# The second MLP's output product, by Strassen's scheme instead of directly

## The chip, the cores and the metric

The kernel runs on one core of a Trainium2 chip. The metric is the device time of one execution in microseconds (us), as a median of runs. TensorE (PE) multiplies matrices, VectorE (DVE) and ScalarE (ACT) do elementwise work and read the results from PSUM, GpSimd (POOL) does elementwise work in SBUF and issues some DMAs, and SyncE (SP) issues most DMAs. Every engine works through its own queue in order.

## What is computed

Attention with a small set of packed queries in the middle, then two MLPs in a row, all in float32 (the weights arrive as float64 words and are converted on the chip):

```
p_packed = softmax(p k^T / 8) v                    # 8 batches, 8 heads, 32 packed rows, head size 64
x  = softmax(q p_packed^T / 8) p_packed            # -> 4608 tokens x 512
h  = x @ w_in                                      # 512 -> 2048
g  = where(h >= 1, h, where(h <= -1, 0, (h + 1)**2 / 4))
y  = g @ w_out                                     # 2048 -> 512
h2 = y @ w2_in                                     # 512 -> 2048
g2 = h2 * sigmoid(h2)
out = g2 @ w2_out                                  # 2048 -> 512
```

## The kernel before

Every float32 product is made of three passes: each operand is split into a high part (ScalarE's cast to the type that TensorE multiplies) and a low part (VectorE subtracts the high part from the value), and TensorE adds high x high, high x low and low x high (`PASSES`) in PSUM.

The program is one list of events, each with a position (`ev`, `at`), sorted and issued in that order; the order of an engine's queue is that of the list. Attention and the first MLP fill 256 steps, up to some 770 us. In the midst of them the input weights of the second MLP are prepared: by pairs of 128 rows (`a_first` to `a_fourth`, `split_a`) they are added and subtracted as one level of Strassen's scheme in Winograd's form asks, split into high and low, and stored to `a_dram`, seven tiles of 256 KB for each of 8 pairs.

The second MLP goes through 6 blocks of 768 tokens. A block's activations `y` are read as four quarters (two halves of the 512 features by two halves of 384 tokens), summed into seven operands and split (`b_side`, `split_b`). Then, for each of the 8 pairs p of hidden tiles, `b_product` multiplies seven weight sums (`load_a`, one tile each, loaded some seven products ahead) with the seven operands: 7 x 2 x 3 = 42 matmuls of 384 columns into two banks, out of which `c_sum` adds the four quarters of the hidden tiles (c11, c21, c12, c22: hidden tile 1 or 2, tokens 1 or 2), with VectorE reading one operand from PSUM. `c_sig` and `c_mult` make x * sigmoid(x), `c_hi` and `c_lo` split it, and `b_out` (L784) multiplies it directly with two tiles of the output weights: tokens are the stationary operand, 512 output features the moving one, 36 matmuls of 512 columns per pair, summed over all pairs in six banks, copied out with tokens on the partitions (L794, L796) and stored (L803). The output weights are converted and split during the first blocks (`conv_a`, `conv_b`, `conv_c`) and stay in SBUF.

The large tiles (weights, operands, splits) share one pool of 37 buffers, `big`; a weight sum's tile is 2 KB per partition.

Of the kernel before, what the change touches and what calls it, by code (L numbers as in the profile page):

```python
# [17 lines left out]

# [60 lines left out]
def attention_then_two_mlps(ctx: ExitStack, tc: tile.TileContext, kT, vv, qT, pT, w_in, w_out, w2_in, w2_out, out):  # L79

# [18 lines left out]
    NT = out.shape[0]  # L99
# [10 lines left out]
    TC = TH // P  # L110
# [31 lines left out]
    a_dram = dram.tile([NPR, 7, P, 2, KH * P], F32, name="a_dram")  # L142

# [484 lines left out]

    def split_a(p, w, j, step):

        n = 1 if step is None else 2
        w = w[:, 512 - n * KH * P:]
        t = big.tile([P, 2, n, KH * P], F32R, tag="big", name="a2w")
        lin = t.rearrange("p i j c -> p i (j c)")  # L640
# [24 lines left out]

    def a_fourth(p):
        split_a(p, w_t.pop(("i2", 2 * p)), 3, 3)
        w_t.pop(("i2", 2 * p + 1))

    a_t, yr_t, b_t = {}, {}, {}  # L670

    def load_a(n):
        if n < 7:
            t = big.tile([P, 2, KH * P], F32R, tag="big", name="a2r")
        elif n % 7 in (4, 5):
            t = wk.tile([P, 2, KH * P], F32R, tag="ysb", name="a2r", bufs=2)
# [12 lines left out]
    def split_b(i, j, src):  # L689
        for a in range(KH):  # L690
            t = big.tile([P, 2, TH], F32R, tag="big", name="y2")
            nc.scalar.copy(t[:, 0], src[:, a])
            nc.vector.tensor_tensor(t[:, 1], src[:, a], t[:, 0].bitcast(F32), op=ALU.subtract)
            b_t[i, j, a] = t

    def b_side(i, j):
        b11, b12, b21, b22 = (yr_t[i, k, t] for k in range(2) for t in range(2))
        if j == 0:
            split_b(i, 0, b11)
            nc.vector.tensor_tensor(b11, b12, b11, op=ALU.subtract)  # L700
        elif j == 1:
            t2 = pools["y"].tile([P, KH, TH], F32, tag="yr", name="yt2", bufs=5)
            nc.vector.tensor_tensor(t2, b22, b11, op=ALU.subtract)
            split_b(i, 1, t2)
            yr_t[i, "t2"] = t2
        elif j == 2:
            split_b(i, 2, b21)
        elif j == 3:
            nc.vector.tensor_tensor(b12, b22, b12, op=ALU.subtract)
            split_b(i, 3, b12)  # L710
        elif j == 4:
            split_b(i, 4, b11)
        elif j == 5:
            nc.vector.tensor_tensor(b21, b21, yr_t[i, "t2"], op=ALU.subtract)
            split_b(i, 5, b21)
        else:
            split_b(i, 6, b22)

    bk, sb, c_t = {}, {}, {}

    def b_product(q, j):
        i, p = divmod(q, NPR)
        if j < 2:
            bk[q, j] = bank("ps_h2")
        ps, w = bk[q, j % 2][:, :TH], a_t.pop(7 * q + j)
        n = 0
        for a in range(KH):
            y = b_t[i, j, a] if p + 1 < NPR else b_t.pop((i, j, a))
            for x, k in PASSES:
                nc.tensor.matmul(  # L730
                    ps, w[:, x, a * P:(a + 1) * P], y[:, k, :], start=(n == 0 and j in (0, 1, 3, 4)),
# [7 lines left out]
    def c_sum(q, name):  # L739
        x, y = bk[q, 0][:, :TH], bk.get((q, 1))  # L740
        if name == "p1":
            sb[q, name] = t = tmp(name, 1)
            nc.scalar.copy(t, x)
            return
        y = y[:, :TH]
        ps, other = {
            "u2": (y, "p1"), "u3": (y, "u2"), "c22": (x, "u3"), "c21": (y, "u2"), "c12": (x, "u2"),
        }[name]
        t = tmp(name if name[0] == "u" else "c", 1 if name[0] == "u" else 2)
        nc.vector.tensor_tensor(t, ps, sb[q, other], op=ALU.add)  # L750
# [8 lines left out]
    def c_mult(q, name):
        u, src = c_t[q, name]  # L760
        nc.vector.tensor_tensor(u, src, u, op=ALU.mult)  # L761

    def c_hi(q, name):
        g = big.tile([P, 2, TH], F32R, tag="big", name="g2")
        nc.scalar.copy(g[:, 0], c_t[q, name][0])  # L765
        g_t[q, name] = g

    def c_lo(q, name):
        g = g_t[q, name]
        nc.vector.tensor_tensor(g[:, 1], c_t.pop((q, name))[0], g[:, 0].bitcast(F32), op=ALU.subtract)  # L770

    o_acc = {}

    def b_out(q):
        i, p = divmod(q, NPR)
        order = ((0, 0), (1, 0), (1, 1), (0, 1)) if q + 1 < NPR * NBK else ((0, 0), (1, 1), (1, 0), (0, 1))
        cells = [(f, t, c, x) for f, t in order for c in range(TC) for x in PASSES]
        for f, t, c, (x, k) in cells:
            first, last = p == 0 and f == t, p == NPR - 1 and f != t
            if first and (x, k) == PASSES[0]:  # L780
                o_acc[t, c] = bank("ps_o") if t and c else ps_a.tile([P, DM], F32, tag="acc", name="ps_o")
            ps = o_acc[t, c]
            g, w = g_t[q, f"c{f + 1}{t + 1}"], w_t["o2", 2 * p + f]
            nc.tensor.matmul(  # L784
                ps, g[:, x, c * P:(c + 1) * P], w[:, k, :],
                start=(first and (x, k) == PASSES[0]), stop=(last and (x, k) == PASSES[-1]),
            )
            if last and (x, k) == PASSES[-1]:
                if t and c < 2 and q + 1 < NPR * NBK:
                    osb = big.tile([P, DM], F32, tag="big", name="osb")  # L790
                else:
                    osb = pools["b"].tile([P, DM], F32, tag="osb", name="osb", bufs=3)
                if c == 1 or c == 2 and t:
                    nc.scalar.copy(osb, ps)  # L794
                else:
# [35 lines left out]
    with tc.manual_schedule():  # L831
# [178 lines left out]
        for p in range(NPR):  # L1010
            n = G['ai'] + G['ad'] * p
            for x in range(2):
                key = ("i2", 2 * p + x)
                at(n + 2 * x, load_raw, key)
                at(n + 2 * x + 3, conv_a, key)
                at(n + 2 * x + 4, conv_b, key)
            for x, fn in enumerate((a_first, a_second, a_third, a_fourth)):
                at(n + 8 + x, fn, p)

        def kb(q, j=0):  # L1020
            return NA - 3.95 + 7 * q + j

        for m in range(KF):
            key = ("o2", m)
            n = NA - 8 + m if m < 4 else kb(m // 2 - 1) + 3.5
            ev(n - 4, load_raw, key)
            ev(n, conv_a, key)
            ev(n + (1 if m < 4 else 0.02), conv_b, key)
            ev(n + (2 if m < 4 else 0.04), conv_c, key)
        for i in range(NBK):  # L1030
            n = kb(i * NPR)
            for k in range(2):
                for t in range(2):
                    ev((NA - 31.4 if i == 0 else n - 22) + 2 * k + t, load_y, i, k, t)
            for j in range(7):
                if i == 0:
                    at(NA - 26 + 3 * j, b_side, i, j)
                else:
                    ev(n + 7 * (-2, -1, -1, -1, 0, 0, 0)[j] + 3.6 + 0.01 * j, b_side, i, j)
        for n in range(7 * NPR * NBK):  # L1040
            ev(kb(0, n) - (3 if n < 7 else 6.6) + 0.39, load_a, n)

        chain = {
            1: [(c_sum, "p1", 0)],
            2: [(c_sum, "u2", 0)],
            3: [(c_sig, "c11", 0), (c_mult, "c11", 1), (c_sum, "u3", 2), (c_hi, "c11", 3), (c_lo, "c11", 4)],
            5: [(c_sum, "c22", 0), (c_sig, "c22", 1)],
# [76 lines left out]
```

## Time and profile before

| | us |
|---|---|
| median of 3 runs | 1531.75 (1530.99 to 1532.3) |
| span of the profiled execution, first to last instruction | 1530.2 |
| TensorE busy in it | 1512.8 |
| VectorE, ScalarE, GpSimd busy | 875.1, 743.4, 85.3 |
| mean granted TensorE clock | 0.998 of full speed |

The profiled execution is one of its own; its whole device time isn't given, so its span stands beside the median of the runs, 1.55 us above it. A busy engine is one with an instruction under way; matmuls overlap, so the mean time of one is longer than the distance from one to the next.

### The profile page before, as it was taken

What the parts mean: (1) busy time and instruction counts of PE and PEld (TensorE: products, weight loads), DVE (VectorE), ACT (ScalarE), POOL (GpSimd) and SP (SyncE); (2) the same over time, 40 slices, a digit from 0 to 9 for tenths busy, and PEclk for the clock granted to TensorE, in tenths of its full rate; (3) what the DMA queues carried; (4) which work ended last, traced back from release to release, by engine and by line L of the source; (5) the groups of instructions that cost most, each with busy time, mean ns of one, the idle gap of its engine ahead of it and who ended that gap; (6) DMA issues with size and microseconds to landing.
All of it is one profiled execution on the core that took longest, in us unless ns stands there. A gap on an engine that the chain in (4) does not pass through costs nothing.

```text
span 1530.2 us, 27671 instructions
## 1 busy us (share of the span) xinstructions
PE 1512.8 (99%) x10546; PEld 1380.4 (90%) x10546; DVE 875.1 (57%) x1831; ACT 743.4 (49%) x1665; POOL 85.3 (6%) x132
## 2 busy tenths in 40 slices
PE   8999999999999999999999999999999999999998
PEld 6788999989899899999998989999898989899997
DVE  5886565564746555575666664564364456447343
ACT  4775657565665656666754442343243334224232
POOL 1430000000000000000000010010001001001000
PEclk9999999999999999999999999999999999999999
DMA  9564545252445252432255653535444445445341
GB/s 333 178 222 141 187 132 169 100 166 102 139 157 169 89 182 70 167 116 92 99 179 187 214 165 108 175 122 161 138 137 146 136 147 160 123 151 173 103 138 62
DMA packets 136723, 226.99 MB, mean 148 GB/s; under 512 B 24336, under 2 KB 70416, under 8 KB 136592
## 3 DMA queue, kind: packets, MB, share of 16 engines
q1 hardware_dynamic: 127120, 192.19, 38.5%
q0 software_dynamic: 9472, 33.04, 6.6%
q8 instruction: 84, 1.38, 0.4%
q14 instruction: 47, 0.39, 0.1%
HBM read 186.25 MB, written 38.93 MB: 147 GB/s over the span
## 4 chain that ended last, share of the span: by engine, by line
PE 92%; DVE 2%; ACT 1%; issue 0%; DMA 0%; SPq 0%; DVEq 0%; ACTq 0%
PE ps_o L784 26%; PE ps_y L604 25%; PE ps_h L730 23%; PE ps_h L569 12%; PE ps_wp L497 2%; PE ps_s L420 2%; PE ps_pp L369 1%; PE ps_tr L457 1%; PE ps_wp L485 0%; DVE raw L168 0%; PE ps_s L275 0%; PE ps_et L334 0%; DVE w L169 0%; ACT u L578 0%; DVE u L584 0%
## 5 line engine op out<-in xcount | busy, mean ns | idle before, releaser
L604 PE MATMUL ps_y<-g,w_o 128*128 128x288 f32 x3072 | 459.8, 299 | 2.1 <-POOL g L594 1.8
L604 PEld LDWEIGHTS ps_y<-g,w_o 128*128 128x128 f32 x3072 | 421.3, 189 | 29.5 <-ACT u L578 15.1
L784 PE MATMUL ps_o<-w_o,g 128*128 128x512 f32 x1728 | 401.4, 390 | 0.0
L784 PEld LDWEIGHTS ps_o<-w_o,g 128*128 128x128 f32 x1728 | 324.1, 188 | 65.5
L730 PE MATMUL ps_h<-y,a2r 128*128 128x384 f32 x2016 | 362.6, 337 | 0.0
L730 PEld LDWEIGHTS ps_h<-y,a2r 128*128 128x128 f32 x2016 | 354.7, 188 | 3.7
L750 DVE TENSOR_TENSOR c<-ps_h,u 128x384 f32<-128x384 f32 x144 | 80.3, 558 | 313.0 <-PE ps_h L730 308.0
L756 ACT ACTIVATE s<-c 128x384 f32<-128x384 f32 x144 | 75.8, 526 | 370.1 <-DVE c L750 368.9
L584 DVE SCALAR_TENSOR_TENSOR u<-ps_h,u 128x288 f32<-128x288 f32 x256 | 116.5, 456 | 230.0 <-ACT u L579 229.7
L569 PE MATMUL ps_h<-a,wp 128*128 128x288 f32 x1536 | 245.0, 295 | 1.5 <-DVE u L584 0.6
L578 ACT ACTIVATE u<-ps_h,half 128x288 f32<-128x288 f32 x256 | 128.0, 500 | 206.4 <-PE ps_h L569 194.6
L569 PEld LDWEIGHTS ps_h<-a,wp 128*128 128x128 f32 x1536 | 217.1, 188 | 4.9 <-DVE u L584 1.5
L579 ACT ACTIVATE u<-u 128x288 f32<-128x288 f32 x256 | 113.8, 444 | 8.1
L765 ACT CAST g<-s 128x384 fp32r<-128x384 f32 x192 | 98.2, 512 | 32.2 <-DVE s L761 30.4
L594 DVE TENSOR_TENSOR g<-u,g 128x288 fp32r<-128x288 f32 x240 | 109.0, 454 | 1.4 <-ACT g L588 1.4
L588 ACT CAST g<-u 128x288 fp32r<-128x288 f32 x256 | 106.7, 418 | 2.5 <-PE ps_y L604 2.2
L770 DVE TENSOR_TENSOR g<-s,g 128x384 fp32r<-128x384 f32 x192 | 102.2, 553 | 4.8
L761 DVE TENSOR_TENSOR s<-c,s 128x384 f32<-128x384 f32 x144 | 79.1, 549 | 0.0
L803 POOL DMA_DIRECT2D out<-osb x40 | 21.4, 542 | 710.6 <-DVE osb L796 710.1
L553 POOL DMA_DIRECT2D win<-win_dram x48 | 25.7, 536 | 535.1 <-PE ps_wp L497 122.9
L151 DVE TENSOR_TENSOR wp<-ps_wp,wp 128x512 fp32r<-128x512 f32 x64 | 41.5, 685 | 10.7 <-ACT wp L150 10.4
L162 ACT ACTIVATE raw<-raw 128x512 f32<-128x512 f32 x64 | 42.7, 676 | 9.3 <-DMA raw<-w_out 5.5
(102 smaller groups left out, 942.1 us busy)
## 6 DMA issues: line engine op xcount, KB each, us to landing
a2r<-a_dram SPq DMA_DIRECT2D x336, 256.0 KB, 3.0
win<-win_dram POOLq DMA_DIRECT2D x48, 512.0 KB, 4.6
raw<-w_in SPq DMA_DIRECT2D x32, 512.0 KB, 7.9
raw<-w_out SPq DMA_DIRECT2D x32, 512.0 KB, 6.0
a_dram<-a2w SPq DMA_DIRECT2D x56, 256.0 KB, 3.3
y_dram<-ysb SPq DMA_DIRECT2D x36, 288.0 KB, 2.5
yr<-y_dram SPq DMA_DIRECT2D x24, 384.0 KB, 6.0
kt<-kT SPq DMA_DIRECT2D x16, 512.0 KB, 5.4
```

The source lines that it names most:

```text
L569: nc.tensor.matmul(ps[:, :HB], w[:, i, o:o + P], a2[:, k, g, :], start=(n == 0), stop=(n == 3 * NG - 1))
L578: nc.scalar.activation(u, h_ps[s][:, :HB], AF.Relu, bias=half, scale=0.5)
L579: nc.scalar.activation(u, u, AF.Square)
L584: nc.vector.scalar_tensor_tensor(u, h_ps.pop(s)[:, :HB], 1.0, u, op0=ALU.max, op1=ALU.min)
L588: nc.scalar.copy(g[:, 0], u_t[s])
L594: eng.tensor_tensor(g[:, 1], u_t.pop(s), g[:, 0].bitcast(F32), op=ALU.subtract)
L604: nc.tensor.matmul(acc["y"][d][:, :HB], w[:, i, d * P:(d + 1) * P], g[:, k], start=(first and n == 0), stop=(last and n == 2),)
L730: nc.tensor.matmul(ps, w[:, x, a * P:(a + 1) * P], y[:, k, :], start=(n == 0 and j in (0, 1, 3, 4)), stop=(n == 3 * KH - 1), skip_group_ch ...
L750: nc.vector.tensor_tensor(t, ps, sb[q, other], op=ALU.add)
L765: nc.scalar.copy(g[:, 0], c_t[q, name][0])
L770: nc.vector.tensor_tensor(g[:, 1], c_t.pop((q, name))[0], g[:, 0].bitcast(F32), op=ALU.subtract)
L784: nc.tensor.matmul(ps, g[:, x, c * P:(c + 1) * P], w[:, k, :], start=(first and (x, k) == PASSES[0]), stop=(last and (x, k) == PASSES[-1]),)
```

## The change

The output product of the second MLP becomes one level of the same scheme as its input product. A block now has two halves. In the first, `h_product` computes the hidden tiles as `b_product` did, two pairs interleaved, into two sets of four banks in turn; the sigmoid products stay in SBUF as float32, in tiles `gs` that two pairs share (20 of them hold all 2048 hidden features of 768 tokens). GpSimd makes the operand sums t1 to t4 from them (`t_sum`). In the second half, for each of the seven products j and each pair p, `o_split` splits the operand (ScalarE, VectorE), three units ahead, and `o_part` multiplies it with a weight sum: weights are now stationary, 384 tokens the moving operand, 2 x 3 matmuls per j and p. The output stands transposed (features on the partitions); `o_sum` adds the quarters out of the banks and stores them, and the host turns the result round. The sums of the output weights are prepared like those of the input weights, within the first MLP, stored to `o_dram`, and loaded again for every block, from nine buffers in a ring. The next block's activations are summed (`b_sum`, GpSimd from the second block on) and split (`b_split`) within the second half of the block before. In the last block the seventh product is done for one half of the output features, then for the other.

```diff
-    NT = out.shape[0]
+    NT = 2 * out.shape[2]
...
+    o_dram = dram.tile([NPR, 7, P, 2, KH * P], F32, name="o_dram")
...
+    U = 7 * NPR
+    RING = 9
+    def unit_h(i, p, j):
+        return 2 * U * i + 14 * (p // 2) + 2 * j + p % 2
+    def unit_o(i, j, p):
+        return 2 * U * i + U + NPR * j + p
-    def load_a(n):
-        if n < 7:
+    def load_a(n, src):
+        if n < RING:
             t = big.tile([P, 2, KH * P], F32R, tag="big", name="a2r")
...
-        nc.sync.dma_start(t.bitcast(F32), a_dram[n // 7 % NPR, n % 7])
+        nc.sync.dma_start(t.bitcast(F32), src)
...
+    def b_split(i, j, a):
+        src = yr_t[i, j][:, a]
+        t = big.tile([P, 2, TH], F32R, tag="big", name="y2")
+        nc.scalar.copy(t[:, 0], src)
+        nc.vector.tensor_tensor(t[:, 1], src, t[:, 0].bitcast(F32), op=ALU.subtract)
+        b_t[i, j, a] = t
+    def b_sum(i, j):
+        eng = nc.gpsimd if i else nc.vector
...
         elif j == 1:
+            eng.tensor_tensor(b11, b12, b11, op=ALU.subtract)
             t2 = pools["y"].tile([P, KH, TH], F32, tag="yr", name="yt2", bufs=5)
-            nc.vector.tensor_tensor(t2, b22, b11, op=ALU.subtract)
+            eng.tensor_tensor(t2, b22, b11, op=ALU.subtract)
...
+    def group_bank(n, name):
+        if n % 2:
+            return ps_a.tile([P, 512], F32, tag="acc", name=name)
+        return bank(name)
+    def h_product(i, p, j):
         if j < 2:
+            bk[i, p, j] = group_bank(5 * i + p // 2, "ps_h2")
...
+    def gs(i, p, name):
+        if (i, p // 2, name) not in gs_t:
+            gs_t[i, p // 2, name] = big.tile([P, 2, TH], F32, tag="big", name="gs")
+        return gs_t[i, p // 2, name][:, p % 2]
...
+    def c_mult(key, name):
+        u, src = c_t.pop((key, name))
+        nc.vector.tensor_tensor(u, src, u, op=ALU.mult)
+    def t_sum(i, p, name):
+        b11, b12, b21, b22 = (gs(i, p, f"c{n}") for n in (11, 12, 21, 22))
+        dst, x, y = {
+            "t1": (gs(i, p, "t1"), b12, b11),
+            "t3": (b12, b22, b12),
+            "t2": (b11, b22, gs(i, p, "t1")),
+            "t4": (b21, b21, b11),
         }[name]
+        nc.gpsimd.tensor_tensor(dst, x, y, op=ALU.subtract)
+    OPERAND = ("c11", "c11", "c21", "c12", "t1", "c21", "c22")
+    def o_split(i, j, p):
+        src = gs(i, p, OPERAND[j])
         g = big.tile([P, 2, TH], F32R, tag="big", name="g2")
+        nc.scalar.copy(g[:, 0], src)
+        nc.vector.tensor_tensor(g[:, 1], src, g[:, 0].bitcast(F32), op=ALU.subtract)
+        go_t[i, j, p] = g
+    def o_part(i, j, p, d, w):
+        if p == 0 and j < 2:
+            bk[i, 0, d, j] = group_bank(5 * i + 4, "ps_o")
+        ps, g = bk[i, 0, d, j % 2][:, :TH], go_t[i, j, p]
+        for n, (x, k) in enumerate(PASSES):
             nc.tensor.matmul(
-                ps, g[:, x, c * P:(c + 1) * P], w[:, k, :],
+                ps, w[:, x, d * P:(d + 1) * P], g[:, k, :], start=(p == 0 and n == 0 and j in FIRST),
...
+    def o_sum(i, name):
+        for d in range(KH):
...
+                c_sum((i, 0, d), name)
+            if name[0] == "c":
...
+                eng = nc.gpsimd if i + 1 < NBK else nc.sync
...
         for p in range(NPR):
+            for kind, n in (("i2", G['ai'] + G['ad'] * p), ("o2", G['ai'] + G['ad'] * p + 12)):
...
+        def bu(n, rank, fn, *args):
+            ev(K0 + n + 0.4 + 0.01 * rank, fn, *args)
+        H_CHAIN = (
+            (0, 0, c_sum, "p1"), (2, 0, c_sum, "u2"), (4, 0, c_sig, "c11"), (5, 1, c_mult, "c11"),
+            (6, 0, c_sum, "u3"), (8, 0, c_sum, "c22"), (9, 2, c_sig, "c22"), (10, 3, c_mult, "c22"),
+            (10, 0, c_sum, "c21"), (11, 2, c_sig, "c21"), (12, 3, c_mult, "c21"),
+            (12, 0, c_sum, "c12"), (13, 2, c_sig, "c12"), (14, 3, c_mult, "c12"),
+        )
+        O_CHAIN = ("p1", "u2", "c11", "u3", "c22", "c21", "c12")
...
+                    n = unit_o(i - 1, j, 0)
+                    bu(n + 1, 20, b_sum, i, j)
+                    for a in range(KH):
+                        bu(n + 3 + 2 * a, 10, b_split, i, j, a)
...
+                for x, name in enumerate(("t1", "t3")):
+                    bu(b + 15, 20 + x, t_sum, i, p, name)
+                for j in range(7):
+                    n = unit_o(i, j, p)
+                    ev(K0 + n + 0.37, o_product, i, j, p)
+                    bu(n - 3, 5, o_split, i, j, p)
+                    if j in (0, 2):
+                        bu(n - 3, 21, t_sum, i, p, "t2" if j == 0 else "t4")
...
+                ev(K0 + n - (3 if n < RING else RING - 0.4) + 0.39, load_a, n, src)
```

A unit in this schedule (`unit_h`, `unit_o`) is one product of one pair: six matmuls.

## Rows read from the trace of the kernel before

**Rows 1.** The page: busy time, share of the span and instructions of each engine.
```profile
PE 1512.8 (99%) x10546; PEld 1380.4 (90%) x10546; DVE 875.1 (57%) x1831; ACT 743.4 (49%) x1665; POOL 85.3 (6%) x132
```
**Rows 2.** Stretches: length, each engine's busy time, then granted clock, DMA share, GB/s.
```profile
115.00:770.00 655.00, 654.20 (x5861) 609.68 (x5860) 382.95 (x900) 402.32 (x953) 25.68 (x48) 1.00 0.40 133
1036.00:1161.00 125.00, 125.00 (x628) 113.44 (x627) 65.70 (x126) 42.02 (x89) 4.25 (x8) 1.00 0.46 145
```
**Rows 3.** The chain of waits in the second MLP: start us, us, what.
```profile
1045.64 7.38 PE ps_h L730 x42
1053.03 8.20 PE ps_o L784 x36
```
**Rows 4.** Groups of instructions by line and form: busy us, mean ns, idle before.
```profile
L784 PE MATMUL ps_o<-w_o,g 128*128 128x512 f32 x1728 | 401.4, 390 | 0.0
L730 PE MATMUL ps_h<-y,a2r 128*128 128x384 f32 x2016 | 362.6, 337 | 0.0
L770 DVE TENSOR_TENSOR g<-s,g 128x384 fp32r<-128x384 f32 x192 | 102.2, 553 | 4.8
```
**Rows 5.** VectorE in order of time, 784 to 786 us: start, duration.
```profile
784.58 0.55 DVE L761 TENSOR_TENSOR s<-c,s 128x384 f32<-128x384 f32 x1
785.05 0.55 DVE L770 TENSOR_TENSOR g<-s,g 128x384 fp32r<-128x384 f32 x1
```
**Rows 6.** GpSimd in order of time, 59 to 61 and 80 to 90 us.
```profile
59.90 0.80 POOL L594 TENSOR_TENSOR g<-u,g 128x288 fp32r<-128x288 f32 x1 [2.60 <-ACT g L588]
...
89.35 1.28 POOL L208 TENSOR_TENSOR w_o<-w,w_o 128x512 fp32r<-128x512 f32 x1 [1.28 <-ACT w_o L206]
```
**Rows 7.** VectorE in order of time, 105 to 112 us.
```profile
105.92 0.44 DVE L594 TENSOR_TENSOR g<-u,g 128x288 fp32r<-128x288 f32 x1
...
110.01 1.56 DVE L594 TENSOR_TENSOR g<-u,g 128x288 fp32r<-128x288 f32 x1
```
**Rows 8.** GpSimd in order of time, 108 to 111 us.
```profile
109.98 1.27 POOL L208 TENSOR_TENSOR w_o<-w,w_o 128x512 fp32r<-128x512 f32 x1 [0.44 <-ACT w_o L206]
```
**Rows 9.** VectorE in order of time, 62.8 to 68.8 us.
```profile
63.26 1.52 DVE L168 TENSOR_SCALAR raw<-raw 128x512 uint32<-128x512 uint32 x1
64.87 1.13 DVE L169 SCALAR_TENSOR_TENSOR w_in<-raw 128x512 uint32<-128x512 uint32 x1
65.92 1.51 DVE L168 TENSOR_SCALAR raw<-raw 128x512 uint32<-128x512 uint32 x1
67.47 1.18 DVE L169 SCALAR_TENSOR_TENSOR w<-raw 128x512 uint32<-128x512 uint32 x1
```
**Rows 10.** GpSimd in order of time, 62.8 to 68.8 us.
```profile
64.45 0.99 POOL L594 TENSOR_TENSOR g<-u,g 128x288 fp32r<-128x288 f32 x1
65.41 1.74 POOL L208 TENSOR_TENSOR w_o<-w,w_o 128x512 fp32r<-128x512 f32 x1
67.11 2.20 POOL L594 TENSOR_TENSOR g<-u,g 128x288 fp32r<-128x288 f32 x2
```
**Rows 11.** A stretch of 2 us in the second MLP, columns as in rows 2.
```profile
1052.00:1054.00 2.00, 2.00 (x11) 1.81 (x10) 1.84 (x5) 1.01 (x2) 0.00 (x0) 1.00 0.79 260
```
**Rows 12.** Tile a2w: durations in ns, least/median/most, first and last start.
```profile
L643 SPq DMA_DIRECT2D a_dram<-a2w x56: 327/575/998, 180.2 to 692.7; - x56
...
L151 DVE TENSOR_TENSOR a2w<-w,a2w x24: 419/684/693, 179.5 to 691.4; 128x512 fp32r<-128x512 f32 x16, 128x256 fp32r<-128x256 f32 x8
```
**Rows 13.** DMA issues by line: KB each, median us from issue to landing.
```profile
a2r<-a_dram SPq DMA_DIRECT2D x336, 256.0 KB, 3.0
...
out<-osb SPq DMA_DIRECT2D x4, 256.0 KB, 2.4
```
**Rows 14.** The end of the kernel in order of time.
```profile
1519.71 4.70 PE L784 MATMUL ps_o<-w_o,g 128*128 128x512 f32 x20
...
1525.04 1.28 ACT L794 COPY osb<-ps_o 128x512 f32<-128x512 f32 x2 [2.73 <-DMA out<-osb]
```

More of the change, by code (lines that the diff above doesn't have):

```diff
@@ L730, in b_product @@
                 nc.tensor.matmul(
-                    ps, w[:, x, a * P:(a + 1) * P], y[:, k, :], start=(n == 0 and j in (0, 1, 3, 4)),
+                    ps, w[:, x, a * P:(a + 1) * P], y[:, k, :], start=(n == 0 and j in FIRST),
                     stop=(n == 3 * KH - 1), skip_group_check=True,
@@ L759, in c_mult @@
[L759 to L763, printed above, removed]
-        g = big.tile([P, 2, TH], F32R, tag="big", name="g2")
[L765 to L783, printed above, removed]
+        b, other = SUMS[name]
@@ new lines, in c_sum, with c_sig @@
+        t = tmp(name, 2) if name[0] == "u" else tmp("c" if len(key) == 2 else "os", 4 if len(key) == 2 else 3)
+        nc.vector.tensor_tensor(t, bk[*key, b][:, :TH], sb[key, other], op=ALU.add)
+        sb[key, name] = t
+    def gs(i, p, name):
+        if (i, p // 2, name) not in gs_t:
+            gs_t[i, p // 2, name] = big.tile([P, 2, TH], F32, tag="big", name="gs")
+        return gs_t[i, p // 2, name][:, p % 2]
+    def c_sig(key, name):
+        src = bk[*key, 0][:, :TH] if name == "c11" else sb[key, name]
+        u = gs(*key, name)
+        nc.scalar.activation(u, src, AF.Sigmoid)
+        c_t[key, name] = (u, src)
@@ new lines, in o_part, with o_product @@
+                stop=(p == NPR - 1 and n == 2), skip_group_check=True,
+            )
+    def o_product(i, j, p):
+        if i == NBK - 1 and j == 6:
+            if p == NPR - 1:
+                for d in range(KH):
+                    for x in range(NPR):
+                        o_part(i, j, x, d, a_t[unit_o(i, j, x)])
+            return
+        w = a_t.pop(unit_o(i, j, p))
+        for d in range(KH):
+            o_part(i, j, p, d, w)
+        go_t.pop((i, j, p))
+    def o_sum(i, name):
+        for d in range(KH):
+            if name == "c11":
+                sb[(i, 0, d), name] = t = tmp("os", 3)
+                if d:
+                    nc.vector.tensor_copy(t, bk[i, 0, d, 0][:, :TH])
+                else:
+                    nc.scalar.copy(t, bk[i, 0, d, 0][:, :TH])
+            else:
+                c_sum((i, 0, d), name)
+            if name[0] == "c":
+                h, t = int(name[1]) - 1, int(name[2]) - 1
+                eng = nc.gpsimd if i + 1 < NBK else nc.sync
+                r = (KH * h + d) * P
+                eng.dma_start(out[r:r + P, t, i * TH:(i + 1) * TH], sb.pop(((i, 0, d), name)))
@@ L1010, in attention_then_two_mlps @@
         for p in range(NPR):
[L1011 to L1029, printed above, removed]
+            for kind, n in (("i2", G['ai'] + G['ad'] * p), ("o2", G['ai'] + G['ad'] * p + 12)):
+                for x in range(2):
+                    key = (kind, 2 * p + x)
+                    at(n + 2 * x, load_raw, key)
+                    at(n + 2 * x + 3, conv_a, key)
+                    at(n + 2 * x + 4, conv_b, key)
+                for x, fn in enumerate((a_first, a_second, a_third, a_fourth)):
+                    at(n + 8 + x, fn, kind, p)
@@ new lines, in attention_then_two_mlps @@
+        K0 = NA - 3.95
+        def bu(n, rank, fn, *args):
[6 more added lines that the diff above has]
+        )
@@ L1040, in attention_then_two_mlps @@
[L1040 to L1047, printed above, removed]
-            6: [(c_sum, "c21", 0), (c_sig, "c21", 1), (c_mult, "c22", 2), (c_hi, "c22", 3)],
-            7: [(c_sum, "c12", 0), (c_sig, "c12", 1), (c_mult, "c21", 2), (c_lo, "c22", 3)],
-            8: [(c_mult, "c12", 1), (c_hi, "c21", 2)],
-            9: [(c_lo, "c21", 1), (c_hi, "c12", 2), (c_lo, "c12", 3)],
-        }
@@ L1053, in attention_then_two_mlps @@
-        for q in range(NPR * NBK):
-            for j in range(7):
-                ev(kb(q, j) + 0.37, b_product, q, j)
-            ev(kb(q + 1, 3) + 0.9, b_out, q)
-            for j, fns in chain.items():
-                for fn, name, x in fns:
-                    ev(kb(q, j) + 0.4 + 0.01 * x, fn, q, name)
+                    at(NA - 26 + 3 * j, b_sum, i, j)
+                    for a in range(KH):
+                        at(NA - 26 + 3 * j, b_split, i, j, a)
+                else:
+                    n = unit_o(i - 1, j, 0)
+                    bu(n + 1, 20, b_sum, i, j)
+                    for a in range(KH):
+                        bu(n + 3 + 2 * a, 10, b_split, i, j, a)
@@ new lines, in attention_then_two_mlps @@
+            for p in range(NPR):
+                b = unit_h(i, p, 0)
+                for j in range(7):
+                    ev(K0 + unit_h(i, p, j) + 0.37, h_product, i, p, j)
+                for n, rank, fn, name in H_CHAIN:
+                    bu(b + n, rank, fn, (i, p), name)
+                for x, name in enumerate(("t1", "t3")):
+                    bu(b + 15, 20 + x, t_sum, i, p, name)
+                for j in range(7):
+                    n = unit_o(i, j, p)
[3 more added lines that the diff above has]
+                        bu(n - 3, 21, t_sum, i, p, "t2" if j == 0 else "t4")
@@ L1061, in when @@
+            for j, name in enumerate(O_CHAIN):
+                bu(unit_o(i, j, NPR - 1), 0, o_sum, i, name)
+            for n, src in (
+                *((unit_h(i, p, j), a_dram[p, j]) for p in range(NPR) for j in range(7)),
+                *((unit_o(i, j, p), o_dram[p, j]) for j in range(7) for p in range(NPR)),
+            ):
+                ev(K0 + n - (3 if n < RING else RING - 0.4) + 0.39, load_a, n, src)
         def when(n, rank, fn, step):
@@ L1122 @@
     r = run_bass_kernel_spmd(nc, [arrays], core_ids=[0])
-    return r.results[0]["out"]
+    y = r.results[0]["out"].reshape(dm, 2, B, S // 2)
+    return np.ascontiguousarray(y.transpose(2, 1, 3, 0)).reshape(B * S, dm)
```

124 lines of the change are left out of this document (42 added, 82 removed).

## Prediction

> **What bounds the kernel now.** I read the page's busy times first: TensorE is busy 1512.8 of 1530.2 us [rows 1]. Busy time can hide stalls, so the next view is the table by stage: from 115 to 770 us (first MLP) TensorE is idle 0.8 us in 655, and in a block of the second MLP (1036 to 1161) not at all, at a granted clock of 1.00 [rows 2]. VectorE has 65.7 of 125 us there, ScalarE 42, GpSimd 4. The chain of waits then shows what the second MLP's time is made of: 7.38 us for the 42 products of its first half, 8.20 us for the 36 of its second, and so on, 48 times, with nothing between [rows 3]. So every matmul cycle counts, other engines only if they come to hold TensorE up. The profiled span is 1530.2 us; the median of the runs is 1531.75, so I add 1.55 us for what lies around the span.
>
> **The products.** The 36 products of 512 columns per pair (1728 in all [rows 4]) go, 8.20 us each time: 48 x 8.20 = 393.6 us. In come 6 blocks x 7 products x 8 pairs x 2 halves x 3 passes = 2016 products of 128x128 by 384, the form of the first half (2016 there too [rows 4]), at 7.38 / 42 = 0.1757 us: 354.2 us. Gain: **39.4 us**. Banks come in two sets of four used in turn, and a bank's sum has three units to be read in the first half, seven in the second; nothing there is tighter than before, where TensorE waited for none. I call a unit six products, 1.054 us; a block has 112, 0 to 55 the first product, 56 to 111 the second, 118.1 us if nothing stalls.
>
> **The operands of the second product.** Before, each pair cost VectorE 13 operations of 384 columns, ScalarE 9. Now it is 16 and 12, and GpSimd gets four subtractions per pair (t1 to t4), and in blocks 0 to 4 also four of 768 columns for the next block's activations. One VectorE operation lasts 0.55 us [rows 4], but in a row they start 0.47 us apart [rows 5]. The second half asks VectorE for one split per unit plus a quarter of one for the next block, about 0.6 us of 1.054: it would fit alone. GpSimd's lone operations take 0.80 us for 288 columns and 1.28 for 512 [rows 6]; on that line 384 columns are 1.00 us and 768 are 1.81.
>
> They don't run side by side. A VectorE subtraction of two SBUF tiles takes 0.44 us alone and 1.56 when it starts with a GpSimd operation, ending 0.32 after it [rows 7, 8]: it stood still until GpSimd was done. In a longer meeting the two alternate, and GpSimd is stretched too: its four operations from 64.45 to 69.31 us would take 3.68 alone, so 1.18 us went to the four VectorE operations that they met, 0.30 each [rows 9, 10]. For 384 columns I take: a held-up VectorE operation ends 0.42 us after GpSimd's, and one pair of them takes 1.30 us, more than a unit.
>
> The Trainium skill, "SBUF — State Buffer", section "Who interferes with whom", says the same of a VectorE instruction with two SBUF inputs and a GpSimd one that reads SBUF: whoever issues first holds the shared port for its whole instruction. The trace agrees on the hold. By its whole-instruction hold a pair would cost 1.00 + 0.47, not 1.30, and the time would be about 1559 us instead of 1545; I go by the rows.
>
> **Where they meet.** The splits are queued three units ahead of their product. Around unit 53 VectorE's queue has the last pairs' sums and sigmoid products, the splits os(0,p) and from unit 61 os(1,p). GpSimd's queue in the same stretch is t2(0..3), t1(6), t2(4), t3(6), t1(7), t2(5), t3(7), t2(6), t2(7), then two of 768 columns: 12 x 1.00 + 2 x 1.81 = 15.6 us. t2(p) overwrites what os(0,p) reads, so it comes after it, and os(1,p) reads t2(p). Set t = 0 at the start of unit 53. The sum after unit 53 can start at 1.1 us; with a multiply behind it, os(0,0) ends at 1.1 + 2 x 0.47 + 0.55 = 2.6. The first four t2 each wait for their split while VectorE does a multiply and a split between them: 4 x 1.00 and about 3.0 of gaps, t = 9.6. Eight more GpSimd operations, each with one VectorE operation in between, 8 x 1.30: 20.0. The two wide ones, 2 x 2.11: 24.2. os(1,4), held behind the last, is there at 24.7 with 0.1 for the signal. TensorE wants it for the second product of unit 68, at 15 x 1.054 + 0.18 = 16.0. **Stall 8.7 us**, spread over units 57 to 68. Behind a held-up split stand all later splits, the next block's splits and the sums of the banks; TensorE waits for those in order. Then t4(0..7) meet os(2,p) and two more of the next block's splits: VectorE has three units in hand, I get 1.0 us. The later wide ones at units 81 and 97 find VectorE far enough ahead: 0. So 9.7 us in each of blocks 0 to 4; the last block has no wide operations and no next splits, and the same working gives 4. **Sum 5 x 9.7 + 4 = 52.5 us.** These idle pieces are under 2 us each; I cost no clock to them, as the granted clock is 1.00 in the stages shown.
>
> **Weights and queues.** The sums of the output weights move into the first MLP: 16 conversions (they leave the second MLP, where they were covered), 32 half-width sums, 32 splits and 56 stores. At 0.42 us for 256 columns and 0.68 for 512 [rows 12], a conversion counted as two wide operations, VectorE gets 32 x 0.42 + 24 x 0.68 + 8 x 0.42 + 32 x 0.68 = 55 us more, on 383 of 655 [rows 2], and ScalarE, with 48 operations, under 33, on 402; the same chain for the input weights runs there eight times now with TensorE idle 0.8 us in all. I take 1 us, with 0 and 5 as bounds. It goes past SP's loads of that stage; an issue there takes 0.33 to 1.0 us [rows 12], and the loads are queued steps ahead. In the second MLP SP issues one load of 256 KB per unit instead of seven per 15.6 us: 249 GB/s, with activations and output 275. TensorE ran at this pace in the first halves before, with 260 GB/s at a DMA share of 0.79 [rows 11], but then had a pause. 275 would be 0.84 of the engines; a load lands in 3.0 us [rows 13] and has 8.6 units, 9 us: cost 0. Were 260 the limit, a block would take 32.5 MB / 260 = 125 us, 7 more than its products, but the stalls above already stretch it to 128.
>
> **The tail.** Before, TensorE ends at about 1524.4 and the span at 1530.2: copies waiting for a buffer until 1526.3, then a store [rows 13, 14]. After, half of the last sums go out under the other half's products; one sum of 0.56, one issue, 2.4 us to land: about 1.1 us less.
>
> 1531.75 - 39.4 + 52.5 + 1.0 - 1.1 = 1544.8: **1545 us**, 0.9% slower. (Runs spread over 1.3 us; 0.2%, 3 us, is what can be told from no change.)
>
> **The rivals.**
> (a) No hold between these operations, GpSimd and VectorE run in parallel. For it: the held ones seen are 288 and 512 wide and few. Then GpSimd's queue, each operation at its own 1.00 or 1.81 us, ends its wide pair at t = 19.2; the next block's second split waits for it, os(1,7) is queued behind that on both engines and is there at 21.0, where unit 71 asks for it at 19.2: 1.8 us a block, 9 in all: 1531.75 - 39.4 + 9 - 0.1 = **1501**, faster. The change gains while the stall is under 7.3 us a block; that is the point that decides.
> (b) The hold is real but VectorE gets in more than one operation per GpSimd one (its next starts before the last ends [rows 5]). All of GpSimd's 15.6 us must still lie before os(1,7), which stands behind the wide pair; with 22 VectorE operations at 0.30 that is t = 2.6 + 15.6 + 6.6 = 24.8 against the 18 x 1.054 + 0.18 = 19.2 at which unit 71 asks for it: 5.6 us a block, 2 in the last: 1531.75 - 39.4 + 30 - 0.1 = **1522**, faster. Against it: the strict alternation of rows 9 and 10.
> (c) The hold lasts longer than I read (0.47 us, an operation's whole distance, added per pair instead of 0.30: 14 x 0.17 x 5 and 2 in the last block, 14 us more: 1559), or waits between neighbouring pairs come on top (two pairs share a tile, so a split of the one could be made to wait for the other's GpSimd operation, some 0.5 us four times a block): 12 to 14 us a block: **1557 to 1570**.
> (d) The weight stream can't be kept up: 7 us a block only shows where (a) or (b) holds, and would bring those to **1540**; against it, 260 GB/s left a fifth of the engines' time free [rows 11].
>
> **Chances.** As worked out 0.42; (c) 0.17; (d) 0.06; (b) 0.22; (a) 0.13. The forecast's own range is 1532 to 1557; with (a) to (c) the range is 1500 to 1572, which leaves some 0.15 out. Faster: (a), (b) and a little of the forecast's low end, 0.35; same 0.05; slower 0.60.
>
> **What would show it.** Second products of 384 columns at 0.176 us; TensorE idle of 8 to 10 us a block, all near the change from first to second product, released by VectorE's split; VectorE splits of over 1 us there and about 0.55 later; GpSimd subtractions at 1.3 us there and 1.0 elsewhere; nothing released by a load. I am wrong if TensorE is idle under 3 us a block (no hold), if the idle pieces lie over the whole second half, or if DMA is their releaser.

## The result, and the profile after

The changed kernel takes 1543.07 us (median of 4 runs, 1541.52 to 1544.31), the kernel before 1531.37 beside it: ratio 1.0079 [1.0064 to 1.0093], 0.8% slower. The profiled span is 1541.6 us against 1530.2, 11.4 more.

The page first, columns as in [rows 1]:
```profile
PE 1488.3 (97%) x10834; PEld 1398.6 (91%) x10834; DVE 1092.0 (71%) x2051; ACT 800.2 (52%) x1825; POOL 349.7 (23%) x344
```
TensorE has 24.5 us less to do and takes 11.4 longer: it now waits. The stretches say where (columns as in [rows 2]: the first MLP, one block of the second, the change from its first product to its second):
```profile
115.00:770.00 655.00, 653.72 (x5855) 608.84 (x5854) 421.52 (x985) 421.21 (x993) 25.51 (x48) 1.00 0.51 167
1161.80:1289.00 127.20, 120.44 (x674) 115.94 (x673) 98.89 (x154) 50.97 (x113) 50.01 (x44) 1.00 0.79 256
1090.00:1135.00 45.00, 38.15 (x200) 33.62 (x199) 44.98 (x54) 21.96 (x51) 31.84 (x25) 1.00 0.66 202
```
The first MLP is untouched by its new work. In the 45 us around the change VectorE is busy without a break and TensorE isn't. The chain of waits from 1034 to 1163 us, against [rows 3], shows what VectorE does there:
```profile
1034.57 55.13 PE ps_h L725 x318
...
1098.45 3.86 DVE g L777 x3
1102.30 1.28 DVE y L683
1103.59 2.55 DVE g L777 x2
...
1129.41 3.14 DVE g L777 x3
...
1132.59 29.24 PE ps_o L785 x167
```
A split takes 1.28 us of the chain where TensorE uses one per 1.04; for 43 us the chain runs mostly through VectorE. TensorE itself, in order of time (the bracket is the idle time before the piece and its releaser):
```profile
1092.65 1.38 PE L785 MATMUL ps_o<-g,a2r 128*128 128x384 f32 x7
1094.30 1.32 PE L785 MATMUL ps_o<-g,a2r 128*128 128x384 f32 x6 [0.27 <-DVE g L777]
...
1104.91 2.60 PE L785 MATMUL ps_o<-g,a2r 128*128 128x384 f32 x12 [1.24 <-DVE g L777]
...
1114.24 11.72 PE L785 MATMUL ps_o<-g,a2r 128*128 128x384 f32 x66 [0.77 <-DVE g L777]
1126.77 5.63 PE L785 MATMUL ps_o<-g,a2r 128*128 128x384 f32 x30 [0.81 <-DVE g L777]
1132.59 17.63 PE L785 MATMUL ps_o<-g,a2r 128*128 128x384 f32 x100 [0.20 <-DVE g L777]
```
GpSimd in the same stretch, in order of time:
```profile
1092.34 1.02 POOL L769 TENSOR_TENSOR gs<-gs 128x384 f32<-128x384 f32 x1 [8.05 <-DVE g L777]
...
1098.06 11.51 POOL L769 TENSOR_TENSOR gs<-gs 128x384 f32<-128x384 f32 x9 [0.49 <-DVE g L777]
1109.53 2.14 POOL L692 TENSOR_TENSOR yr<-yr 128x768 f32<-128x768 f32 x1
1111.74 2.02 POOL L694 TENSOR_TENSOR yt<-yr 128x768 f32<-128x768 f32 x1
```
Nine subtractions in 11.51 us are 1.28 each, the pace of the splits: one for one. A subtraction that finds no split or multiply under way takes 1.02 (the first row). When the second wide one ends, at 1113.76, VectorE is free again and TensorE goes on half a microsecond later. The groups by line and form, against [rows 4], and the loads, against [rows 13]:
```profile
L785 PE MATMUL ps_o<-g,a2r 128*128 128x384 f32 x2016 | 375.0, 341 | 35.6 <-DVE g L777 35.6
L725 PE MATMUL ps_h<-y,a2r 128*128 128x384 f32 x2016 | 351.7, 334 | 1.4 <-DVE u L743 1.4
L777 DVE TENSOR_TENSOR g<-gs,g 128x384 fp32r<-128x384 f32 x336 | 266.1, 841 | 0.0
L769 POOL TENSOR_TENSOR gs<-gs 128x384 f32<-128x384 f32 x192 | 225.3, 1192 | 403.6 <-ACT p L739 186.1 <-DVE gs L759 116.1 <-DVE g L777 87.9
```
```profile
a2r<-a_dram SPq DMA_DIRECT2D x336, 256.0 KB, 3.4
a2r<-o_dram SPq DMA_DIRECT2D x336, 256.0 KB, 3.0
```
The profile names no load as the releaser of a product; in block 0 two waits are for loads all the same (under "Terms mis-sized" below). The end, in order of time, against [rows 14]:
```profile
1536.80 1.03 PE L785 MATMUL ps_o<-g,a2r 128*128 128x384 f32 x5
...
1537.86 0.56 DVE L743 TENSOR_TENSOR os<-ps_o,u 128x384 f32<-128x384 f32 x1 [3.61 <-PE ps_o L785]
1538.45 0.33 SPq L816 DMA_DIRECT2D out<-os  x1
```

**The account.** What a block costs unstalled is read below, from a version that doesn't stall: 116.8 us, 0.1738 us a product. In the changed kernel's chain of waits the blocks start at 770.26, 906.00, 1034.57, 1161.83, 1289.03 and 1416.24, and the last product ends at 1537.84. The first holds 6.5 us of the first MLP's last products. Less 116.8 each, the blocks lose 12.5, 11.8, 10.5, 10.4, 10.4 and 4.8 us, together 60.4. The products gain 48 x 15.58 - 4032 x 0.1738 = 47.0. The second MLP starts 0.1 us later and the tail is 2.0 shorter (3.8 against 5.8): -47.0 + 60.4 + 0.1 - 2.0 = 11.5, the 11.4 of the spans. TensorE's idle in the groups, 35.6 and 1.4 us, is less than the 60.4: a piece without a gap can be slow too (the 12 matmuls at 1104.91 take 2.60 us, 2.09 at 0.1738 each), so the account goes by lengths and not by idle time.

### The profile page after: what moved, and what is told of

Same layout as the page of the kernel before. It is cut to its first block, busy times and chain, and to the rows that moved or that the text cites. A ratio compares the mean times of both kernels' runs of the same rounds, so it can differ in the third digit from the quotient of the medians.

```text
span 1541.6 us, 29864 instructions
## 1 busy us (share of the span) xinstructions
PE 1488.3 (97%) x10834; PEld 1398.6 (91%) x10834; DVE 1092.0 (71%) x2051; ACT 800.2 (52%) x1825; POOL 349.7 (23%) x344
## 4 chain that ended last, share of the span: by engine, by line
PE 78%; DVE 14%; ACT 2%; issue 1%; DMA 0%; DVEq 0%; ACTq 0%
PE ps_y L592 25%; PE ps_h L725 22%; PE ps_o L785 14%; PE ps_h L557 12%; DVE g L777 8%; DVE y L683 2%; PE ps_wp L485 2%; PE ps_s L408 2%; DVE gs L759 1%; DVE c L743 1%; PE ps_pp L357 1%; PE ps_tr L445 1%; DVE raw L156 0%; PE ps_wp L473 0%; PE ps_s L263 0%
## 5 line engine op out<-in xcount | busy, mean ns | idle before, releaser
L785 PE MATMUL ps_o<-g,a2r 128*128 128x384 f32 x2016 | 375.0, 341 | 35.6 <-DVE g L777 35.6
L785 PEld LDWEIGHTS ps_o<-g,a2r 128*128 128x128 f32 x2016 | 347.7, 189 | 62.0 <-DVE g L777 61.9
L725 PE MATMUL ps_h<-y,a2r 128*128 128x384 f32 x2016 | 351.7, 334 | 1.4 <-DVE u L743 1.4
L769 POOL TENSOR_TENSOR gs<-gs 128x384 f32<-128x384 f32 x192 | 225.3, 1192 | 403.6 <-ACT p L739 186.1
L777 DVE TENSOR_TENSOR g<-gs,g 128x384 fp32r<-128x384 f32 x336 | 266.1, 841 | 0.0
L776 ACT CAST g<-gs 128x384 fp32r<-128x384 f32 x336 | 149.2, 509 | 2.3 <-POOL gs L769 2.1
L754 ACT ACTIVATE gs<-c 128x384 f32<-128x384 f32 x144 | 75.8, 526 | 132.5 <-DVE c L743 131.9
L743 DVE TENSOR_TENSOR c<-ps_h,u 128x384 f32<-128x384 f32 x144 | 80.1, 556 | 36.7 <-PE ps_h L725 35.7
L759 DVE TENSOR_TENSOR gs<-c,gs 128x384 f32<-128x384 f32 x144 | 93.1, 657 | 9.6 <-ACT gs L754 9.6
L682 ACT CAST y<-yr 128x384 fp32r<-128x384 f32 x72 | 36.1, 510 | 53.7 <-POOL yr L704 40.1
L754 ACT ACTIVATE gs<-ps_h 128x384 f32<-128x384 f32 x48 | 23.5, 492 | 72.3 <-PE ps_h L725 72.3
```

Of the source, the lines that this page charges most:

```text
L725: nc.tensor.matmul(ps, w[:, x, a * P:(a + 1) * P], y[:, k, :], start=(n == 0 and j in FIRST), stop=(n == 3 * KH - 1), skip_group_check=True,)
L769: nc.gpsimd.tensor_tensor(dst, x, y, op=ALU.subtract)
L776: nc.scalar.copy(g[:, 0], src)
L777: nc.vector.tensor_tensor(g[:, 1], src, g[:, 0].bitcast(F32), op=ALU.subtract)
L785: nc.tensor.matmul(ps, w[:, x, d * P:(d + 1) * P], g[:, k, :], start=(p == 0 and n == 0 and j in FIRST), stop=(p == NPR - 1 and n == 2), s ...
```

## The experiments

My theory: a GpSimd operation that reads SBUF and a VectorE operation with two SBUF inputs hold each other up, so that splits come at 1.28 us while GpSimd has sums to do. Its rivals: GpSimd is merely slow, and TensorE waits for its results; VectorE has too much to do; the order in which sums and splits are queued is what matters.

**Which sums, and whose.** Three runs give GpSimd's sums to VectorE, all (e1), those of the next block's activations (e2) or those of the hidden activations (e7); the first edit is in e1 and e2, the second in e1 and e7:
```diff
     def b_sum(i, j):
-        eng = nc.gpsimd if i else nc.vector
+        eng = nc.vector
...
-        nc.gpsimd.tensor_tensor(dst, x, y, op=ALU.subtract)
+        nc.vector.tensor_tensor(dst, x, y, op=ALU.subtract)
```


> All operand sums (t1 to t4 and the next block's activation sums) move from GpSimd to VectorE, order unchanged. Theory (a GpSimd operation holds VectorE's two-input operation, so a sum on GpSimd takes about 0.8 us from VectorE, and on VectorE 0.47 for 384 columns, 0.9 for 768): TensorE's stall falls from about 10 us a block to 3 or 4, all at the change from first to second product, where VectorE has some 41 operations in 18 units; 1510 to 1516 us. Rival (VectorE simply has too much work in the second half, GpSimd helps it): 18 us more a block on VectorE, 1590 us or more.

> Only the next block's activation sums (four operations of 768 columns) move to VectorE; t1 to t4 stay on GpSimd. Theory (hold): the two wide ones cost 2 x 2.1 us at the change and only 2 x 0.9 on VectorE, some 2 to 3 us less stall in each of five blocks: about 1529 us. Rival (VectorE has too much work): 3.6 us more on VectorE a block, about 1560 us.

> The changed kernel with t1 to t4 on VectorE and only the activation sums left on GpSimd (the counterpart of e2). Theory (hold): e1 plus two holds of about 1.6 us at the change in five blocks, less the 1.8 us that VectorE saves there: 1513 to 1522 us. Rival (VectorE's work is the limit, each operation taken from it helps): faster than e1 by 5 x 3.6 us, about 1495 us.

Measured: e1 1512.47 us, 0.9881 [0.9865 to 0.9898] of the kernel before; e2 1532.13, 1.0011 [1.0001 to 1.0022]; e7 1521.5, 0.9937 [0.9917 to 0.9957]. Against 1543.07 that is 30.6, 10.9 and 21.6 us less: the two kinds of sums nearly add up (32.5 against the 30.6 of both at once). Groups of e1:
```profile
L785 PE MATMUL ps_o<-g,a2r 128*128 128x384 f32 x2016 | 364.1, 337 | 15.4 <-DVE g L777 14.8
...
L777 DVE TENSOR_TENSOR g<-gs,g 128x384 fp32r<-128x384 f32 x336 | 173.5, 550 | 1.9 <-ACT g L776 1.9
```
Every split is back at 550 ns with the same sums done: that VectorE has too much to do explains at most what is left, 15.4 us of TensorE's idle in this row and 27.4 us by the time of e5 below. It lies in the first of the same units, 57 to 62, where VectorE's sums still stand in front of its splits.

**Writing without reading.** e3 leaves out each sum of hidden activations and puts two fills of the same tile in its place, still on GpSimd:
```diff
-        nc.gpsimd.tensor_tensor(dst, x, y, op=ALU.subtract)
+        nc.gpsimd.memset(dst, 0.0)
+        nc.gpsimd.memset(dst, 0.0)
```


> GpSimd's subtractions t1 to t4 are each replaced by two memsets of the same tile (the operand sums are left out): GpSimd's queue, its writes and the waits for its writes stay, only its reads of SBUF go; the activation sums stay on GpSimd. Theory (hold between GpSimd's reads and VectorE's two-input operations): VectorE's splits fall to 0.55 us except beside the wide sums, stall 2 to 4 us a block, 1500 to 1512 us. Rival 1 (any GpSimd operation holds VectorE): splits stay held, some 0.8 to 0.9 us each, 1535 us or more. Rival 2 (no hold, VectorE's work is what is late): as the changed kernel, 1543 us.

Measured: 1489.51 us, 0.9732 [0.9712 to 0.9751], below what I expected. GpSimd in e3, then VectorE there, in order of time:
```profile
1082.59 0.42 POOL L770 MEMSET gs<- 128x384 f32 x1
1082.97 2.07 POOL L692 TENSOR_TENSOR yr<-yr 128x768 f32<-128x768 f32 x1
1085.12 2.04 POOL L694 TENSOR_TENSOR yt<-yr 128x768 f32<-128x768 f32 x1
```
```profile
1078.54 0.55 DVE L683 TENSOR_TENSOR y<-yr,y 128x384 fp32r<-128x384 f32 x1
1079.01 0.55 DVE L778 TENSOR_TENSOR g<-gs,g 128x384 fp32r<-128x384 f32 x1
1081.84 5.73 DVE L778 TENSOR_TENSOR g<-gs,g 128x384 fp32r<-128x384 f32 x5 [2.27 <-ACT g L777]
```
Beside the fills a split takes 0.55 us; beside the two wide sums, which read, five take 5.73. By the Trainium skill ("SBUF — State Buffer", section "Who interferes with whom"), a VectorE instruction with two SBUF inputs contends with a GpSimd one that reads SBUF, not with one that only writes; these rows agree. The same page of the Trainium skill says in its section "SBUF: two separate sides" that whichever of the two starts first has the port for its whole instruction. In the changed kernel the split behind the second wide sum does end only 0.4 us after it, at 1114.18, but the pair takes 1.28 us, not 1.02 + 0.47, and the row decides the price. The run alone doesn't price the hold, since two fills, 0.42 us each, are also shorter than a sum.

The changed kernel's own trace shows which VectorE operations are held. Where a GpSimd sum is already under way and has 0.3 us or more to go, the sums that take one operand from PSUM (L743, 43 of them) last 0.54 to 0.56 us, as they do elsewhere; the splits of the next block's activations (L683, 20 of them) last 1.36 instead of 0.55. One input isn't always free of it, though: in [rows 9] L168, which has one, takes 1.52 us against a median of 0.42 for its line.

**The order.** e5 is e1 with the sums moved away from the change: t2 after the product that frees its tile, t3 of the last two pairs and t4 later, the next block's sums and splits eight units on. e6 is the same order with the sums back on GpSimd.
```diff
-                    n = unit_o(i - 1, j, 0)
+                    n = unit_o(i - 1, j, 0) + 8
...
-                    bu(b + 15, 20 + x, t_sum, i, p, name)
+                    bu(b + 15 + (11 if name == "t3" and p >= NPR - 2 else 0), 20 + x, t_sum, i, p, name)
...
-                        bu(n - 3, 21, t_sum, i, p, "t2" if j == 0 else "t4")
+                        bu(unit_o(i, 0, p) + 3 if j == 0 else unit_o(i, 2, 0) + 5 + 2 * p, 21, t_sum, i, p, "t2" if j == 0 else "t4")
```


> As e1, and what isn't needed yet moves away from the change: t2 six units later, t3 of the last two pairs eleven later, t4 one every two units from unit 77 on, the next block's sums and splits eight units later. Theory (what is left in e1 is VectorE's queue at the change): VectorE then has at most two operations, 0.94 us, per unit of 1.04, and the stall is 0 to 1 us a block: 1488 to 1496 us, faster than the kernel before by 2.3 to 2.8%. Rival (VectorE has too much work in all): as e1.

> The order of e5 with all operand sums back on GpSimd: tells the order's share from the engine's. Theory (hold): the ten GpSimd operations from unit 57 to 69 now meet one VectorE split per unit, each pair 1.28 us against a unit of 1.04, and the two wide ones at unit 73 cost about 2 us more; 4 to 6 us stall a block where the changed kernel had 10 and e5 nearly none: 1507 to 1522 us. Rival (only the order mattered, not the engine): as e5, 1485 us.

Measured: e5 1485.09 us, 0.9703 [0.9688 to 0.9717]; e6 1539.9, 1.0057 [1.0037 to 1.0078], so order alone is worth 3 us and I had hoped for over 20. The chain of waits of e5 is the [rows 3] picture again:
```profile
894.76 58.24 PE ps_h L725 x336
953.00 2.28 PE ps_o L785 x13
...
955.31 56.26 PE ps_o L785 x323
1011.57 58.24 PE ps_h L725 x336
```
116.8 us for the 672 products of a block. Its stretch, columns as in [rows 2], and its page:
```profile
1040.00:1160.00 120.00, 119.98 (x692) 119.64 (x692) 97.39 (x195) 53.11 (x117) 4.29 (x8) 1.00 0.86 279
```
```profile
PE 1465.2 (99%) x10834; PEld 1399.7 (94%) x10834; DVE 1069.6 (72%) x2263; ACT 803.2 (54%) x1825; POOL 85.1 (6%) x132
```
VectorE does 212 operations more than in the changed kernel and is busy 22.4 us less: what GpSimd took off it, it lost standing still. In e6 the delayed sums are held up too, and now arrive late themselves:
```profile
L785 PE MATMUL ps_o<-g,a2r 128*128 128x384 f32 x2016 | 379.1, 342 | 28.6 <-DVE g L777 25.8 <-ACT g L776 1.8
...
L777 DVE TENSOR_TENSOR g<-gs,g 128x384 fp32r<-128x384 f32 x336 | 256.8, 806 | 26.4 <-ACT g L776 26.4
L769 POOL TENSOR_TENSOR gs<-gs 128x384 f32<-128x384 f32 x192 | 236.9, 1258 | 383.3 <-ACT p L739 185.4 <-DVE gs L759 184.2 <-PE ps_h L725 10.2
...
L776 ACT CAST g<-gs 128x384 fp32r<-128x384 f32 x336 | 151.2, 510 | 50.5 <-POOL gs L769 50.5
```
ScalarE's cast waits 50.5 us for GpSimd's sums, against 2.1 before the move: the rival that GpSimd's results come late holds in this order, and not in the changed kernel's. No run tells how much of e6's time is the one and how much the other.

**The hold without anyone waiting.** To separate the hold from waiting for results, e8 and e10 keep e5 and add GpSimd subtractions whose result nobody reads: e8 192 of them on a tile of their own, e10 144 (in the second half, for the first three operands) that read the low part just split, so that they can't run ahead.
The edit of e10:
```diff
+    def idle_read(i, j, p):
...
+        nc.gpsimd.tensor_tensor(t[:, 0], t[:, 1], go_t[i, j, p][:, 1].bitcast(F32), op=ALU.subtract)
...
+                    if j < 3:
+                        bu(n - 3, 22, idle_read, i, j, p)
```


> e5 (all sums on VectorE) plus, on GpSimd, as many 384-wide subtractions as the changed kernel has t sums (192), at their places in the order, of one tile of its own that no other engine touches: no result is waited for, so only the meeting of the two engines is added. Theory (hold): each takes about 0.8 us from VectorE wherever VectorE is pressed, 10 to 13 us stall a block: 1540 to 1565 us. Rival (the changed kernel's stall is that of late GpSimd results): as e5, 1485 us.

> e5 plus, on GpSimd, 24 subtractions of 384 columns a block that nobody waits for, each reading the low part that a split of j = 0, 1 or 2 has just written (so each runs when that split is done, unlike in e8, where GpSimd ran ahead of the order): 144 in all, between units 53 and 77, where the changed kernel has 20 and two wide ones. Theory (hold): each takes about 0.8 us from VectorE, which has some 23 us of work in these 25: 14 to 16 us stall a block, 1565 to 1585 us. Rival (the changed kernel's stall is that of late GpSimd results): as e5, 1485 us.

Measured: e8 1495.26 us, 0.9766 [0.9746 to 0.9785], far below expectation; e10 1584.79, 1.0355 [1.0334 to 1.0375]. GpSimd in e8, in order of time, shows what went wrong with it:
```profile
896.10 1.07 POOL L825 DMA_DIRECT2D out<-os  x2 [7.24 <-DVE os L743]
897.18 32.05 POOL L778 TENSOR_TENSOR idle<-idle 128x384 f32<-128x384 f32 x32
```
Bound to nothing, 32 run in one go as soon as an output store lets the queue pass, and that falls into the first half, where VectorE has time to spare (its multiplies at L759 take 692 ns instead of e5's 549, and TensorE waits 5.6 us for VectorE). e8 is 10.2 us over e5, 0.05 for each operation. In e10 they run where they were meant to. TensorE there, in order of time, and the groups:
```profile
977.33 1.32 PE L794 MATMUL ps_o<-g,a2r 128*128 128x384 f32 x6 [0.43 <-DVE g L786]
979.09 1.33 PE L794 MATMUL ps_o<-g,a2r 128*128 128x384 f32 x6 [0.44 <-DVE g L786]
```
```profile
L786 DVE TENSOR_TENSOR g<-gs,g 128x384 fp32r<-128x384 f32 x336 | 256.9, 792 | 0.0
...
L778 POOL TENSOR_TENSOR idle<-idle,g 128x384 f32<-128x384 f32 x144 | 171.3, 1190 | 413.9 <-DVE g L786 412.3
```
With no instruction waiting for GpSimd's results, TensorE's units come 1.76 us apart: a held split of 1.29 and a sum of 0.47 on VectorE. The run is 99.7 us over e5's, of which a mean granted clock of 0.997 against 1.000 makes some 5: 0.66 to 0.69 per operation, more than the 0.47 that VectorE needs for such a subtraction itself. This settles the hold.

**Where it costs nothing, and the best version.** e9 is e5 with the first nine weight sums loaded eight units ahead instead of three; e11 is e9 with t1 and t3 of the first six pairs on GpSimd, in the first half:
```diff
-                ev(K0 + n - (3 if n < RING else RING - 0.4) + 0.39, load_a, n, src)
+                ev(K0 + n - (8 if n < RING else RING - 0.4) + 0.39, load_a, n, src)
```
```diff
-        nc.vector.tensor_tensor(dst, x, y, op=ALU.subtract)
+        eng = nc.gpsimd if name in ("t1", "t3") and p < NPR - 2 else nc.vector
+        eng.tensor_tensor(dst, x, y, op=ALU.subtract)
```

> e5 with the first nine weight loads of the second MLP queued eight units ahead instead of three; in e5 TensorE waited 1.3 us for two of them, behind a store in SyncE's queue. Theory: that wait goes, 1 to 2 us less than e5, 1483 to 1484 us. Rival (the buffers for them come free no earlier): as e5, 1485 us.

> e9 with t1 and t3 of the first six pairs, 12 subtractions a block, back on GpSimd: they lie in the first half, where VectorE has some 10 us of work in 14.6. Theory (a hold costs only where VectorE is pressed): as e9, 1482 to 1487 us. Rival (every hold reaches TensorE): 12 x 0.8 us a block, 1540 us.

Measured: e9 1483.8 us, 0.9692 [0.9675 to 0.9708]; e11 1483.97, 0.9696 [0.968 to 0.9712]: the same. In e11 the 72 sums take 1.06 us each on GpSimd and TensorE's waits stay at 0.2 us. e9 is 3.1% faster than the kernel before and 59 us faster than the changed one: about the 60.4 us of the account.

## Why the prediction came out

**The stall, right in kind, place and almost in size.** In the block shown, unit 53 starts at 1034.57 + 55.13 = 1089.70, after 318 matmuls. Counted from there, the working's five times (2.6, 9.6, 20.0, 24.2 and 24.7 us) came out at 2.6, 9.6, 19.9, 24.1 and 24.5. TensorE wanted the last split at 15 x 1.043 + 0.17 = 15.8 and goes on with the second product of unit 68 at 1114.24, 24.5: a stall of 8.7 us, as forecast. The pair of operations I put at 1.30 us, from four meetings of other shapes, is 1.28. The sign I named, 8 to 10 us of idle a block, holds by length (10.4); the profile's idle pieces of this block come to 6.9.

**Terms mis-sized.** (1) *t4*: I took 1.0 us; 1.7 were measured, at units 79 and 84. (2) *Last block*: I took 4; 4.8 were measured. (3) *The first loads*, put at 0: another 2.0 us of block 0 lie in its first half, where TensorE stops before units 7 and 8, at 784 and 786 us. The profile names VectorE's sums out of the banks; the same two stops in e5 bear another name. TensorE in the changed kernel, then in e5, in order of time:
```profile
784.85 1.30 PE L725 MATMUL ps_h<-y,a2r 128*128 128x384 f32 x6 [0.73 <-DVE u L743]
```
```profile
784.22 1.28 PE L725 MATMUL ps_h<-y,a2r 128*128 128x384 f32 x6 [0.77 <-DMA a2r<-a_dram]
786.04 14.28 PE L725 MATMUL ps_h<-y,a2r 128*128 128x384 f32 x81 [0.53 <-DMA a2r<-a_dram]
```
In the changed kernel weight loads land at 784.71 and 786.68, 0.14 us before TensorE goes on each time, and VectorE's sums happen to end within 0.1 us of them; in e5 the second sum ends at 786.10, after TensorE has gone on. e9, which only queues the first loads earlier, has neither stop: its block 0 loses 0.1 us where that of e5 loses 1.9. My 8.6 units for a load to land hold from the tenth on; the first nine are queued three units ahead, some of them behind two stores of `y`. (4) *The clock*, costed at nothing. In block 1 the same stall is followed by this, columns as in [rows 2]:
```profile
976.00:985.60 9.60, 6.53 (x30) 5.01 (x30) 9.60 (x8) 3.49 (x8) 9.12 (x6) 1.00 0.45 136
985.60:987.60 2.00, 1.94 (x7) 1.94 (x8) 2.00 (x6) 2.00 (x6) 0.00 (x0) 0.62 0.47 135
987.60:989.60 2.00, 2.00 (x9) 2.00 (x8) 2.00 (x3) 2.00 (x6) 1.26 (x1) 0.52 0.37 131
989.60:991.60 2.00, 2.00 (x13) 2.00 (x13) 0.68 (x3) 1.87 (x5) 1.02 (x1) 1.00 0.45 143
```
After a stretch with TensorE busy 68% the granted clock is 0.62 and 0.52 over 4 us, so most of the time at the lower level, 1.2 GHz; block 1 is 1.3 us longer than block 2 for it. Of the five blocks with this stall the other four, with much the same pieces, show no fall. Together the blocks lose 60.4 us where I had 52.5.

**The products.** I took 7.38 / 42 = 0.1757 us from a half that alternated with products of 512 columns. Undisturbed (e5) it is 58.24 / 336 = 0.1733 in the first half and 0.174 in the second: 47.0 gained where I had 39.4. This error and that of the stall, 7.6 and 7.9 us, cancelled by luck; 1545 against 1543.07 is closer than the terms were.

**Covered work.** The weight sums in the first MLP (1 us taken, 0.1 measured) were hidden, and so were the loads after the first nine: even e5, which has no stall to stretch the block, draws 279 GB/s at a share of 0.86 and waits for none of them. The tail gave 2.0 us for 1.1; its own pieces, 0.56, an issue of 0.33 to 1.0 and 2.4, leave 3.3 to 4.0 of 5.8, so 1.8 to 2.5 less, and the 1.1 didn't follow from them. Two other sums of the working are off without moving the forecast: the line through GpSimd's two times gives 1.01 and 1.83 us, not 1.00 and 1.81, and the 1540 of rival (d) lies between 1534 (six times 7 us alone) and 1543 (with the 9 of (a) on top).

**The rivals.** (a), no hold, fell with e3, e8 and e10; (b), several VectorE operations per GpSimd one, with the 1.28 us pace of both engines; (c), a longer hold, with the same 1.28, and its waits between neighbouring pairs with the 2.1 us that ScalarE's casts wait for GpSimd's sums in the whole run; (d), the weight stream, with e5.

## What to carry to other kernels

An elementwise operation given to a second engine isn't free help where the two hold each other up: look in the profile for how long both take when they meet, and compare the loss with what the operation costs the busy engine itself (here about 0.7 against 0.47 us; nothing in e11, where the busy engine has time to spare). Then ask what stands in that engine's queue in front of the work that is waited for: engine and order together were worth 58 us here, the engine alone 31, the order alone 3. Price an instruction from a stretch where nothing alternates with it, or keep the difference as a bound. And where two things end at the same moment, a profile's releaser can be the wrong one: a version that moves only one of them tells.

## What the hardware showed beyond that

When both queues are full, GpSimd and VectorE take strict turns, one operation each, at 1.28 us a pair for 128x384: more than GpSimd's 1.02 and less than the 1.49 of the two in a row. A VectorE sum with one operand in PSUM isn't held (0.54 to 0.56 us beside a GpSimd sum). A fill on GpSimd neither holds nor is held (0.42 us, beside splits of 0.55). And of five stalls of nearly the same length and pattern one was followed by TensorE's lower clock, the other four not.
